# Wider zero rows from alternate partitions, and x and dy on two DMA queues, in a decode step with its gradients

## The chip, the cores and the metric

The kernel runs on one core of a Trainium2 chip. The metric is device time in microseconds (us), the median over runs of the whole program. The core has a matrix engine (PE), VectorE (DVE), ScalarE (ACT), GpSimd (POOL) and SyncE (SP), and 16 DMA engines that serve three queues here: SP's and ACT's (hardware queues, `q1` and `q10` in the profile) and POOL's (the software queue, `q0`).

## What is computed

One decode step of a parallel block, forward and backward. Four batch rows of width 512 are normalised. Attention with 32 query heads, 8 key/value heads of width 128 and a cache of 4096 positions uses only the last W = 1024 of them. A gated feed-forward part of width 1792 runs beside it.

```python
def _A_ref(x, k_cache, v_cache, wq, wo):
    W = min(4096, max(256, Sk // 4))
    q = (x @ wq).reshape(B, Sq, Hq, Dh)...
    k = jnp.repeat(k_cache[:, :, Sk - W:, :], rep, axis=1)
    v = jnp.repeat(v_cache[:, :, Sk - W:, :], rep, axis=1)
    p = _softmax(jnp.einsum("bhqd,bhkd->bhqk", q, k) * (Dh ** -0.5))
    o = jnp.einsum("bhqk,bhkd->bhqd", p, v)
    return ... @ wo
def _B_ref(x, w_gate, w_up, w_down):
    return (_gelu(x @ w_gate) * (x @ w_up)) @ w_down
xn = _layernorm(x)
out = x + _A_ref(xn, ...) + _B_ref(xn, ...)
# outputs: out, and the gradients of x, k_cache, v_cache, wq, wo, w_gate, w_up, w_down for grad_out
```

The gradients of the two caches have the caches' full shape (4 x 8 x 4096 x 128 in bf16); three quarters of them, the positions before the window, are zeros that the kernel has to write.

## The kernel before

**Head.** x and dy (the incoming gradient) are loaded by ACT's queue, each row repeated 32 times so that all 128 partitions are filled (L128). Layer norm on DVE and ACT gives `xn_b` and, through four PE transposes, `xnT`. `dyP` is a 32 x 32 block transpose of dy and is copied into `dyBD`, which PE later multiplies with. Small masks and selections (`hsel`, `hsel2`, `selp` and others) are made on DVE from the identity.

**Loads.** SP's queue issues the weights in the order `wg`, `wu`, `wd`, `wq`, `wo`, then the first key tile `ka`, then the first four zero transfers (L266 to L272). The later key and value tiles (`va`, `kb`, `ka`) are loaded from POOL's queue.

**Zeros.** `ztile` (128 partitions of 6 KB) is the source of all zeros. `zeros(n, after)` (L240) issues n transfers from SP's queue, each for two heads of one batch row of one gradient: 2 x 128 rows of 6 KB, 1.5 MB; 32 of them in all. A zero transfer waits for the one two before it, so that two are in flight, and, where `after` is given, for that instruction: the first 4 are free, and of the rest most wait for the landing of a key or value load (2 for `va` of batch 0, 3 for `kb` of batch 1, then 2 and 3 per batch, 4 for the last `va`), 3 for the last softmax and 6 for the last two attention products.

**Feed-forward part** (L253 to L375). `h_ps` = xnT times wg and wu; GELU and its derivative on DVE and ACT with fp32 values `x2`, `ua`, `th`, `h1` in tiles of the pool `ffn`; then the gradients `dwd`, `dwu`, `dwg`. Results are evacuated from PSUM into staging tiles (`stg_tile`, 4 buffers) by ACT or DVE, as `evac` (L82) chooses from a running cost of both, and stored from POOL's queue by `result` (L112).

**Attention** (L377 to L634). Per batch row: `scores` (DVE transposes a key or value tile through `scratch`, two buffers, and PE multiplies), `softmax`, `turned`, `odq` (product with the values, `od_ps`), the load of the next tile, `dvdk` (the gradient of the values or keys: 16 evacuations into two staging tiles, two stores of 1 MB). `get_d` (L452) uses `hsel` and `hsel2` as weights; `selh` is a selection used in `odq`, `selb` one used at the end.

**End** (L636 on). out, the gradient of x, and the gradients of wo and wq, four 1 MB stores each.

The engines' instruction order comes from a scheduler; SP's queue is scheduled by hand, in program order.

Of the kernel before, what the change touches and what calls it, by code (L numbers as in the profile page):

```python
# [11 lines left out]
FP32 = mybir.dt.float32  # L12
BF16 = mybir.dt.bfloat16
U32 = mybir.dt.uint32
P = 128
# [3 lines left out]
def kernel(  # L19
# [24 lines left out]
    nc = tc.nc  # L44

    B, Sq, D = A_x.shape
    _, G, Sk, Dh = A_k_cache.shape
# [4 lines left out]
    K0 = Sk - W  # L52
    F = B_w_gate.shape[1]
    Q = 32
    NQ = P // Q
# [5 lines left out]
    NPB = D // 64  # L61
# [8 lines left out]
    const = ctx.enter_context(tc.tile_pool(name="const", bufs=1))  # L70
# [20 lines left out]
    def t32(out, in_, n):  # L91
        load["dve"] += (130 + n) / 0.96
        nc.vector.transpose(out=out, in_=in_)  # L93

    def pairs(ap):
        return ap.bitcast(U32)

    def scratch():
        return scrp.tile([P, 1024], U32, name="scr", tag="scr")

    def stg_tile():
        return stage.tile([P, 4096], BF16, name="stg", tag="stg")

    def store(eng, out, in_, kind, apart, **kw):

        d = eng.dma_start(out=out, in_=in_, **kw)  # L106
        for k in apart:
            tc.declare_no_dep(d.ins, group=k, reason="stores write disjoint parts of the outputs")
        tc.add_to_no_dep_group(kind, d.ins)
        return d  # L110
# [4 lines left out]
    def mm(out, lhsT, rhs, first=True, last=True, pos=None):  # L115
        kw = {} if pos is None else {"tile_position": pos}
        nc.tensor.matmul(out, lhsT=lhsT, rhs=rhs, start=first, stop=last, **kw)  # L117

    def bank(name, tag="w", shape=(P, 512), dt=FP32):
        pool = {"w": ps_w, "x": ps_x}.get(tag, ps_a)  # L120
        return pool.tile(list(shape), dt, name=name, tag=tag)
# [3 lines left out]

    x_b = const.tile([P, D], BF16, name="x_b")
    dy_b = const.tile([P, D], BF16, name="dy_b")
    for dst, src in ((x_b, A_x), (dy_b, grad_out)):  # L128
        nc.scalar.dma_start(out=dst[:], in_=bass.AP(tensor=src.tensor, offset=src.offset,
                                                  ap=[[0, Q], [D, B], [1, D]]))  # L130

    ident = const.tile([P, P], BF16, name="ident")
    make_identity(nc, ident[:])
# [11 lines left out]
    r0 = rsum[:, 0, :]  # L145
# [3 lines left out]
    def mask(name, n, in_):  # L149
        t_ = const.tile([P, n], FP32, name=name)  # L150
        nc.vector.reduce_sum(out=t_[:], in_=in_, axis=AX.X)
        return t_
# [6 lines left out]
    hm = mask("hm", Q, ident_f[:].rearrange("p (h d) -> p h d", d=4))  # L159
# [5 lines left out]
    TS(out=oms[:], in0=om[:], scalar1=scale, scalar2=None, op0=ALU.mult)  # L165
    gmask_b = const.tile([P, G], BF16, name="gmask_b")
    nc.vector.tensor_copy(out=gmask_b[:], in_=gmask[:])
    hsel = const.tile([P, NQ, Q], BF16, name="hsel")
    nc.vector.tensor_copy(out=hsel[:], in_=hm[:].unsqueeze(1).broadcast_to([P, NQ, Q]))
    hsel2 = const.tile([P, NQ, 4, 8], BF16, name="hsel2")  # L170
    nc.vector.tensor_copy(out=hsel2[:], in_=hm[:].rearrange("p (c r) -> p c r", c=NQ).unsqueeze(2)
                          .broadcast_to([P, NQ, 4, 8]))
    rs2 = const.tile([P, NQ, 4, 8], FP32, name="rs2")
    for c in range(NQ):
        TS(out=rs2[:, c], in0=m8[:].unsqueeze(1).broadcast_to([P, 4, 8]), scalar1=bm[:, c:c + 1], scalar2=None,
# [3 lines left out]
    for a in range(4):  # L179
        TS(out=selp[:, a], in0=rs2[:, :, 0, :], scalar1=amask[:, a:a + 1], scalar2=None, op0=ALU.mult)  # L180

    ZW = K0 // P * Dh
    ztile = const.tile([P, ZW], BF16, name="ztile")
    nc.gpsimd.memset(ztile[:], 0.0)


    stats = const.tile([P, nc.vector.BN_STATS_DIM], FP32, name="stats")
# [13 lines left out]
        nc.tensor.transpose(tps[:, c, :], xn_b[0:Q, c:D:C], ident[0:Q, 0:Q])  # L201
    nc.vector.tensor_copy(out=xnT[:], in_=tps[:])

    dyP = const.tile([P, NPB, Q], U32, name="dyP")
    t32(dyP[:], pairs(dy_b[:]), 256)
    dyBD = const.tile([P, NPB, 2, P], BF16, name="dyBD")
    nc.gpsimd.memset(dyBD[:], 0.0)
    dyPb = dyP[:].bitcast(BF16).rearrange("p n (x r) -> p n r x", r=2)
    for q in quad:
        nc.vector.tensor_copy(out=dyBD[q, :, :, q], in_=dyPb[q])  # L210

# [17 lines left out]
        return d  # L229

    ZG = 2
    zsrc = bass.AP(tensor=ztile.tensor, offset=ztile.offset, ap=[list(ztile[:].ap[0]), [0, ZG], [1, ZW]])
    ztodo = [(og, b, g) for b in range(B) for g in range(0, G, ZG) for og in (out_2, out_3)]
    zdone = []

    def behind(ins, other):
        tc.add_manual_dep(ins, other.name,
                          mybir.DependencyInfo(mybir.DependencyClass.Sync, mybir.DependencyReason.DATA))

    def zeros(n, after=None):  # L240

        for _ in range(n):
            og, b, g = ztodo.pop(0)
            z = store(nc.sync, og[b, g:g + ZG, 0:K0, :].rearrange("g (m j) d -> m g (j d)", m=P), zsrc, "zeros",
                      ["rest"])
            if len(zdone) >= 2:
                behind(z.ins, zdone[-2].ins)
            if after is not None:
                behind(z.ins, after.ins)
            zdone.append(z)  # L250


    with tc.tile_pool(name="ffn", bufs=1) as ffn:  # L253
        wd_sb = ffn.tile([P, FB, D], BF16, name="wd_sb")

        def ft(name, dt=FP32):
            return ffn.tile([P, Q, FB], dt, name=name)
# [1 line left out]
        def flat(t_):  # L259
            return t_[:].rearrange("p f c -> p (f c)")  # L260

        hg, hu, x2, ua, th, h1, gl = (ft(n) for n in ("hg", "hu", "x2", "ua", "th", "h1", "gl"))
        a_b, dhu, dhg = (ft(n, BF16) for n in ("a_b", "dhu", "dhg"))
        wu_sb = ffn.tile([P, C, F], BF16, name="wu_sb")
        wg_sb = ffn.tile([P, C, F], BF16, name="wg_sb")
# [8 lines left out]
        for wsb, t_ in ((wg_sb, hg), (wu_sb, hu)):  # L274
            ps = bank("h_ps", "w", (P, FQ))
# [46 lines left out]
        for fb in range(FB):  # L322
            c = fb % 4
# [4 lines left out]
        for h in range(2):  # L328
            stg = stg_tile()
            for i in range(FB // 2):  # L330
                ps = bank("dwd_ps")
# [7 lines left out]
        for wi, (wsb, dh, og) in enumerate(((wu_sb, dhu, out_7), (wg_sb, dhg, out_6))):  # L339
            dh_f = flat(dh)  # L340
            dhr = stg_tile()
            for a, q in enumerate(quad):
                ps = bank("rep_ps", "w", (P, FQ))
# [9 lines left out]
            for ch in range(4):  # L353
# [5 lines left out]
                for k in range(n7):  # L359
                    for r in range(2):  # L360
                        c = nm % 4
# [4 lines left out]
            for h in range(2):  # L366
                stg = stg_tile()
                for ci in range(2):
                    for a, q in enumerate(quad):
                        ps = bank("dwg_ps", "w", (P, FQ))  # L370
# [6 lines left out]
    with tc.tile_pool(name="mid", bufs=1, reuse_waits="tile") as mid:  # L377
# [3 lines left out]
        selb = mid.tile([Q, 4, P], BF16, name="selb")  # L381
        with tc.tile_pool(name="att", bufs=1, reuse_waits="tile") as att:
# [7 lines left out]
            for k in range(2):  # L390
                bd.append([])
                for u in range(2):
                    t_ = att.tile([P, DPB, NQ, 2, 2, Q], BF16, name=f"bd{k}{u}")
                    nc.gpsimd.memset(t_[:], 0.0)
                    bd[k].append(t_)
            selh = att.tile([P, 4, Q, 4], FP32, name="selh")
            nc.gpsimd.memset(selh[:], 0.0)
            for d4 in range(4):
                nc.gpsimd.tensor_copy(out=selh[:, d4, :, d4], in_=r0)
            nc.gpsimd.tensor_copy(out=selb[:], in_=selh[0:Q].rearrange("p d h e -> p d (h e)"))  # L400
            nc.gpsimd.memset(dqs[:], 0.0)

            q_ps = bank("q_ps", "x", (P, Hq, B))
# [40 lines left out]
            for u in range(2):  # L444
                t32(doX[:, u * 16:(u + 1) * 16, :], do_ps[u][:], 512)
            d4mask = mask("d4mask", 4, r0.rearrange("p (g i) -> p i g", i=rep))
            dM = scratch()[:].bitcast(BF16)[:, 0:512].rearrange("p (b e k) -> p b e k", b=B, e=4)
            for d4 in range(4):
                TS(out=dM[:, :, d4, :], in0=doX[:, :, 0:B].rearrange("p k x -> p x k"), scalar1=d4mask[:, d4:d4 + 1],
                   scalar2=None, op0=ALU.mult)  # L450

            def get_d(ps, u):  # L452
                l_ = hsel[:].rearrange("p a h -> p (a h)") if u == 0 else hsel2[:].rearrange("p c a r -> p (c a r)")
                mm(ps[:].rearrange("p b d -> p (b d)"), l_, dM.rearrange("p b e k -> p (b e k)"))

            spread_rows(1, get_d)

            def refill(k, b):
# [104 lines left out]
            def odq(k, b, pT):  # L563

                ps = bank("od_ps", "x", (P, 2, Dh))
                src = (v_t, k_t)[k][b]
                for j in range(J):
                    for c, q in enumerate(quad):
                        mm(ps[q].rearrange("p g d -> p (g d)"), pT[:, j, :], src[:, 2 * c:2 * c + 2, j, :],
                           j == 0, j == J - 1, (0, Q * c))  # L570
                mk = (om, oms)[k]
                t_ = att.tile([P, Dh], FP32, name="odt", tag=f"odt{k}")
                nc.scalar.activation(out=t_[:], in_=ps[:, 0, :], func=ACT.Copy, scale=mk[:, 0:1])  # L573
                done = STT(out=t_[:], in0=ps[:, 1, :], scalar=mk[:, 1:2], in1=t_[:], op0=ALU.mult, op1=ALU.add)  # L574
                if k == 0:
                    ps = bank("ok_ps", "x", (P, NQ, 4, 2))
                    for d4 in range(4):
                        mm(ps[:].rearrange("p c t e -> p (c t e)"), selh[:, d4].rearrange("p h e -> p (h e)"),
                           t_[:, d4 * Q:(d4 + 1) * Q].rearrange("p (t c e) -> p c t e", t=4, c=NQ), d4 == 0, d4 == 3)
                    nc.vector.tensor_copy(out=oK[:, :, b], in_=ps[:].rearrange("p c t e -> p (c t e)"))  # L580
                else:
                    ps = bank("dqr_ps", "x", (P, Dh))
                    mm(ps[:], rsum_f, t_[:])
                    nc.scalar.copy(out=dqr[:, b, :], in_=ps[:])
                    d3 = att.tile([P, DPB, Q], U32, name="d3", tag="d3")
                    t32(d3[:], pairs(dqr[:, b, :]), 64)
                    d3v = d3[:].bitcast(BF16).rearrange("p e (h r) -> p h e r", r=2)
                    for a, q in enumerate(quad):
                        nc.vector.tensor_copy(out=dqs[q, :, :, :, a * B + b], in_=d3v[q])  # L589
                return done  # L590
# [45 lines left out]
        with tc.tile_pool(name="end", bufs=1, reuse_waits="tile") as end:  # L636
# [14 lines left out]
            for n in range(KH):  # L651
                t, e, c = n // 8, n // 4 % 2, n % 4
# [17 lines left out]
            for hc in range(8):  # L670
                for k in range(8):
                    for r in range(2):
                        c = nm % 4
# [38 lines left out]
            for t in range(4):  # L712
                stg = stg_tile()
                for e in range(2):
                    for c, q in enumerate(quad):
                        ps = bank("dwo_ps")
# [6 lines left out]
            for c in range(C):  # L723
                stg = stg_tile()
                for u in range(2):
                    for a, q in enumerate(quad):
                        ps = bank("dwq_ps")
# [34 lines left out]
```

## Time and profile before

| | |
|---|---|
| median of 3 runs | 288.5 us (287.89 to 289.36) |
| profiled execution | 287.67 us, of which the span of instructions is 285.9 us |
| mean granted PE clock | 0.623 |
| busy: PE, DVE, ACT, POOL | 64%, 57%, 43%, 21% of the span |
| DMA | 112.21 MB, mean 392 GB/s; 20979 packets |
| zeros (`out_dram<-ztile`) | 32 transfers of 1536 KB from SP's queue, median 12.7 us from issue to landing |
| stores (`out_dram<-stg`) | 24 of 1024 KB and 6 of 896 KB from POOL's queue, median 14.1 and 10.0 us |

In the profile, times are us from the span's start. A busy row gives an engine's time in instructions; the row DMA in 40 slices gives the mean busy share of the 16 DMA engines in tenths. The chain is the work that ended last, followed back from the last instruction through what released each step. In a timeline row the columns are start, length, engine, line, operation, result<-operands and, in brackets, the idle time before it and what ended it. "SPq", "ACTq" and "POOLq" are the engines' sequencers, where DMAs are issued; a DMA's issue is far shorter than the transfer.

### The profile page before, as it was taken

To read this page: it belongs to the slowest core of one execution; us is meant where nothing else is said; L and a number is where in the kernel's file an instruction comes from. 1 tells how busy PE (TensorE), PEld (TensorE's weight loads), DVE (VectorE), ACT (ScalarE), POOL (GpSimd) and SP (SyncE) were. 2 spreads that over 40 slices of the span, in tenths; PEclk is the share of its full clock that TensorE was granted. 3 is DMA by queue.
4 is the path that set the end of the run, shared out by engine and by line. 5 is a ranking of instruction groups with operands and counts; after the bars stand their busy time and mean duration, and the time that the engine had idled before them with its cause. 6 is when DMAs were issued, how large, how long until landed. Compare 5 with 4: busy or idle time off the path is not lost.

```text
span 285.9 us, 4404 instructions
## 1 busy us (share of the span) xinstructions
PE 183.3 (64%) x1731; PEld 75.1 (26%) x1733; DVE 161.8 (57%) x309; ACT 123.9 (43%) x245; POOL 60.6 (21%) x135
## 2 busy tenths in 40 slices
PE   0022689986935499869955697513769979755660
PEld 0010235423312252424321352201343234201110
DVE  0058975789979653457219553073974042775570
ACT  1004287382010248956823535303607593554560
POOL 8400001047618222313040060200200102011010
PEclk9999997555885555757555555555555575755555
DMA  7999999999999949999999999999999999999995
GB/s 273 420 462 435 398 380 423 419 426 369 390 424 425 376 161 410 378 357 421 407 418 376 423 415 406 420 424 419 403 399 395 414 386 399 391 406 412 415 402 220
DMA packets 20979, 112.21 MB, mean 392 GB/s; under 512 B 1368, under 2 KB 1632, under 8 KB 19296
## 3 DMA queue, kind: packets, MB, share of 16 engines
q1 hardware_dynamic: 10480, 66.32, 56.6%
q0 software_dynamic: 10176, 45.35, 40.6%
q10 hardware_dynamic: 304, 0.27, 0.3%
q8 instruction: 13, 0.21, 0.3%
q14 instruction: 6, 0.05, 0.0%
HBM read 30.93 MB, written 81.01 MB: 391 GB/s over the span
## 4 chain that ended last, share of the span: by engine, by line
PE 22%; DMA 22%; DVE 15%; ACT 4%; issue 4%; POOL 1%; POOLq 0%; DVEq 0%; ACTq 0%
DMA out_dram<-stg 16%; PE kv_ps L117 7%; DVE scr L93 6%; DMA va<-in_A_v_cache_dram 6%; ACT stg L88 3%; PE od_ps L117 3%; PE sc_ps L117 2%; PE ob_ps L117 2%; DVE stg L89 2%; DVE dqs L589 2%; PE dxq_ps L117 2%; DVE wq_sb L93 2%; PE ok_ps L117 1%; PE dwq_ps L117 1%; PE dwo_ps L117 1%
## 5 line engine op out<-in xcount | busy, mean ns | idle before, releaser
L88 ACT CAST stg<-kv_ps 128x512 bf16<-128x512 f32 x118 | 63.6, 605 | 42.3 <-PE kv_ps L117 21.6
L106 POOL DMA_DIRECT2D out_dram<-stg x30 | 19.8, 660 | 157.0 <-ACT stg L88 93.0
L117 PE MATMUL sc_ps<-scr,bd 128*32 128x256 bf16 x256 | 23.5, 391 | 16.3 <-DVE scr L93 16.3
L117 PE MATMUL kv_ps<-dm,spr 32*128 32x256 bf16 x128 | 28.0, 391 | 4.0 <-ACT stg L88 2.4
L117 PE MATMUL kv_ps<-qm,spr 32*128 32x256 bf16 x128 | 24.4, 371 | 7.4 <-ACT stg L88 6.9
L93 DVE STREAM_TRANSPOSE scr<-va 128x1024 uint32<-128x1024 uint32 x16 | 18.8, 1215 | 14.7 <-DMA va<-in_A_v_cache_dram 14.6
L117 PEld LDWEIGHTS <-spr 32*128 32x128 bf16 x256 | 12.2, 101 | 40.0 <-issue 35.6
L117 PEld LDWEIGHTS <-bd 128*32 128x32 bf16 x256 | 7.9, 108 | 27.7 <-issue 26.9
L88 ACT CAST stg<-dwg_ps 128x448 bf16<-128x448 f32 x26 | 12.6, 553 | 5.7 <-PE dwg_ps L117 4.8
L88 ACT CAST stg<-dwo_ps 128x512 bf16<-128x512 f32 x18 | 10.0, 589 | 11.5 <-PE dwo_ps L117 10.2
L117 PE MATMUL dwo_ps<-dy_b,oSP 32*128 32x512 bf16 x32 | 9.9, 549 | 6.8 <-ACT stg L88 5.9
L117 PE MATMUL dwq_ps<-dqSP,xn_b 32*128 32x512 bf16 x32 | 10.5, 588 | 5.8 <-ACT stg L88 5.3
L89 DVE CAST stg<-dwq_ps 128x512 bf16<-128x512 f32 x15 | 9.9, 689 | 6.4 <-DMA out_dram<-stg 3.4
L574 DVE SCALAR_TENSOR_TENSOR odt<-od_ps,oms,odt 128x128 f32<-128x128 f32 x4 | 1.4, 340 | 20.9 <-ACT odt L573 20.9
L89 DVE CAST stg<-kv_ps 128x512 bf16<-128x512 f32 x10 | 6.6, 678 | 10.4 <-PE kv_ps L117 7.4
L88 ACT CAST stg<-dwq_ps 128x512 bf16<-128x512 f32 x17 | 9.3, 587 | 6.4 <-DMA out_dram<-stg 4.5
L226 POOL DMA_DIRECT2D va<-in_A_v_cache_dram x8 | 6.0, 758 | 27.9 <-PE od_ps L117 27.9
L117 PE MATMUL do_ps<-scr,dyBD 128*128 128x512 bf16 x31 | 10.1, 458 | 2.4 <-DVE scr L93 2.0
L201 PE MATMUL tps<-ident,xn_b 32*128 32x32 bf16 x4 | 0.3, 194 | 17.5 <-DVE xn_b L197 17.5
L93 DVE STREAM_TRANSPOSE scr<-ka 128x1024 uint32<-128x1024 uint32 x8 | 9.6, 1228 | 2.3 <-PE sc_ps L117 1.6
L89 DVE CAST stg<-dwo_ps 128x512 bf16<-128x512 f32 x14 | 9.2, 679 | 2.7 <-PE dwo_ps L117 1.4
L117 PEld LDWEIGHTS <-pT 128*32 128x32 bf16 x256 | 9.3, 140 | 5.1 <-ACT pT L88 2.3
(197 smaller groups left out, 322.4 us busy)
## 6 DMA issues: line engine op xcount, KB each, us to landing
out_dram<-ztile SPq DMA_DIRECT2D x32, 1536.0 KB, 12.7
out_dram<-stg POOLq DMA_DIRECT2D x24, 1024.0 KB, 14.1
va<-in_A_v_cache_dram POOLq DMA_DIRECT2D x8, 1024.0 KB, 12.6
out_dram<-stg POOLq DMA_DIRECT2D x6, 896.0 KB, 10.0
wq_sb<-in_A_wq_dram SPq DMA_DIRECT2D x1, 4096.0 KB, 25.0
wo_sb<-in_A_wo_dram SPq DMA_DIRECT2D x1, 4096.0 KB, 33.8
kb<-in_A_k_cache_dram POOLq DMA_DIRECT2D x4, 1024.0 KB, 15.7
ka<-in_A_k_cache_dram SPq DMA_DIRECT2D x2, 1024.0 KB, 31.2
```

Source lines behind the costliest of these rows:

```text
L88: return nc.scalar.copy(out=out, in_=in_)
L89: return nc.vector.tensor_copy(out=out, in_=in_)
L93: nc.vector.transpose(out=out, in_=in_)
L106: d = eng.dma_start(out=out, in_=in_, **kw)
L117: nc.tensor.matmul(out, lhsT=lhsT, rhs=rhs, start=first, stop=last, **kw)
L201: nc.tensor.transpose(tps[:, c, :], xn_b[0:Q, c:D:C], ident[0:Q, 0:Q])
L226: d = eng.dma_start(out=tl[:, hs].rearrange("p g j d -> p g (j d)"), in_=src[b, hs, K0:Sk, :].rearrange("g (m j) d -> m g (j d)", j=J), **kw)
L574: done = STT(out=t_[:], in0=ps[:, 1, :], scalar=mk[:, 1:2], in1=t_[:], op0=ALU.mult, op1=ALU.add)
L589: nc.vector.tensor_copy(out=dqs[q, :, :, :, a * B + b], in_=d3v[q])
```

## The change

x is loaded from the head of SP's queue; dy stays on ACT's queue, alone. `ztile` holds 12 KB per partition, and a zero transfer reads 64 alternate partitions (0, 2, 4 and so on): 2 x 64 rows of 12 KB, the same 1.5 MB. The memory for this comes from tiles that go: the four fp32 feed-forward values share one staging tile, `dyP`, `hsel` and `hsel2` go into scratch tiles (the last two are now made just before their use), and `selh`, four selections of 128 columns, becomes one row pattern of 132 columns that is read at four offsets.

```diff
-    for dst, src in ((x_b, A_x), (dy_b, grad_out)):
-        nc.scalar.dma_start(out=dst[:], in_=bass.AP(tensor=src.tensor, offset=src.offset,
-                                                  ap=[[0, Q], [D, B], [1, D]]))
+    for eng, dst, src in ((nc.sync, x_b, A_x), (nc.scalar, dy_b, grad_out)):
+        eng.dma_start(out=dst[:], in_=bass.AP(tensor=src.tensor, offset=src.offset,
+                                              ap=[[0, Q], [D, B], [1, D]]))
...
-    hsel = const.tile([P, NQ, Q], BF16, name="hsel")
-    nc.vector.tensor_copy(out=hsel[:], in_=hm[:].unsqueeze(1).broadcast_to([P, NQ, Q]))
-    hsel2 = const.tile([P, NQ, 4, 8], BF16, name="hsel2")
-    nc.vector.tensor_copy(out=hsel2[:], in_=hm[:].rearrange("p (c r) -> p c r", c=NQ).unsqueeze(2)
-                          .broadcast_to([P, NQ, 4, 8]))
...
-    ZW = K0 // P * Dh
+    ZP = P // 2
+    ZW = K0 // ZP * Dh
     ztile = const.tile([P, ZW], BF16, name="ztile")
-    nc.gpsimd.memset(ztile[:], 0.0)
+    nc.gpsimd.memset(ztile[:].bitcast(FP32), 0.0)
...
-    dyP = const.tile([P, NPB, Q], U32, name="dyP")
-    t32(dyP[:], pairs(dy_b[:]), 256)
+    dyP = scratch()[:, 0:256].rearrange("p (n x) -> p n x", n=NPB)
+    t32(dyP, pairs(dy_b[:]), 256)
...
-    zsrc = bass.AP(tensor=ztile.tensor, offset=ztile.offset, ap=[list(ztile[:].ap[0]), [0, ZG], [1, ZW]])
+    zsrc = bass.AP(tensor=ztile.tensor, offset=ztile.offset, ap=[[2 * ztile[:].ap[0][0], ZP], [0, ZG], [1, ZW]])
...
-            z = store(nc.sync, og[b, g:g + ZG, 0:K0, :].rearrange("g (m j) d -> m g (j d)", m=P), zsrc, "zeros",
+            z = store(nc.sync, og[b, g:g + ZG, 0:K0, :].rearrange("g (m j) d -> m g (j d)", m=ZP), zsrc, "zeros",
...
-        hg, hu, x2, ua, th, h1, gl = (ft(n) for n in ("hg", "hu", "x2", "ua", "th", "h1", "gl"))
+        hg, hu, gl = (ft(n) for n in ("hg", "hu", "gl"))
+        tmp = stg_tile()[:, 0:4 * 2 * F // NQ].bitcast(FP32).rearrange("p (t f c) -> p t f c", t=4, f=Q)
+        x2, ua, th, h1 = (tmp[:, t] for t in range(4))
...
-            selh = att.tile([P, 4, Q, 4], FP32, name="selh")
+            selh = att.tile([P, P + 4], FP32, name="selh")
             nc.gpsimd.memset(selh[:], 0.0)
-            for d4 in range(4):
-                nc.gpsimd.tensor_copy(out=selh[:, d4, :, d4], in_=r0)
-            nc.gpsimd.tensor_copy(out=selb[:], in_=selh[0:Q].rearrange("p d h e -> p d (h e)"))
+            nc.gpsimd.tensor_copy(out=selh[:, 4:P + 4].rearrange("p (h e) -> p h e", e=4)[:, :, 0], in_=r0)
+            for b in range(B):
+                nc.gpsimd.tensor_copy(out=selb[:, b, :], in_=selh[0:Q, 4 - b:P + 4 - b])
...
-            dM = scratch()[:].bitcast(BF16)[:, 0:512].rearrange("p (b e k) -> p b e k", b=B, e=4)
+            dsc = scratch()[:].bitcast(BF16)
+            dM = dsc[:, 0:512].rearrange("p (b e k) -> p b e k", b=B, e=4)
+            hsel = dsc[:, 512:640].rearrange("p (a h) -> p a h", a=NQ)
+            hsel2 = dsc[:, 640:768].rearrange("p (c a r) -> p c a r", c=NQ, a=4)
+            nc.vector.tensor_copy(out=hsel, in_=hm[:].unsqueeze(1).broadcast_to([P, NQ, Q]))
+            nc.vector.tensor_copy(out=hsel2, in_=hm[:].rearrange("p (c r) -> p c r", c=NQ).unsqueeze(2)
+                                  .broadcast_to([P, NQ, 4, 8]))
```

More of the change, by code (lines that the diff above doesn't have):

```diff
@@ L202 @@
     nc.vector.tensor_copy(out=xnT[:], in_=tps[:])
-    dyP = const.tile([P, NPB, Q], U32, name="dyP")
-    t32(dyP[:], pairs(dy_b[:]), 256)
+    dyP = scratch()[:, 0:256].rearrange("p (n x) -> p n x", n=NPB)
+    t32(dyP, pairs(dy_b[:]), 256)
     dyBD = const.tile([P, NPB, 2, P], BF16, name="dyBD")
     nc.gpsimd.memset(dyBD[:], 0.0)
-    dyPb = dyP[:].bitcast(BF16).rearrange("p n (x r) -> p n r x", r=2)
+    dyPb = dyP.bitcast(BF16).rearrange("p n (x r) -> p n r x", r=2)
     for q in quad:
@@ L452, in get_d @@
             def get_d(ps, u):
-                l_ = hsel[:].rearrange("p a h -> p (a h)") if u == 0 else hsel2[:].rearrange("p c a r -> p (c a r)")
+                l_ = dsc[:, 512:640] if u == 0 else dsc[:, 640:768]
                 mm(ps[:].rearrange("p b d -> p (b d)"), l_, dM.rearrange("p b e k -> p (b e k)"))
@@ L577, in odq @@
                     for d4 in range(4):
-                        mm(ps[:].rearrange("p c t e -> p (c t e)"), selh[:, d4].rearrange("p h e -> p (h e)"),
+                        mm(ps[:].rearrange("p c t e -> p (c t e)"), selh[:, 4 - d4:P + 4 - d4],
                            t_[:, d4 * Q:(d4 + 1) * Q].rearrange("p (t c e) -> p c t e", t=4, c=NQ), d4 == 0, d4 == 3)
```

## The prediction

> **What bounds the kernel now.** I read the page's DMA rows first, since they say whether any engine matters at all. In the third section a row is a queue, its packets, its bytes and the time of its packets as a share of 16 engines' span.
>
> ```profile
> DMA  7999999999999949999999999999999999999995
> GB/s 273 420 462 435 398 380 423 419 426 369 390 424 425 376 161 410 378 357 421 407 418 376 423 415 406 420 424 419 403 399 395 414 386 399 391 406 412 415 402 220
> ...
> q1 hardware_dynamic: 10480, 66.32, 56.6%
> q0 software_dynamic: 10176, 45.35, 40.6%
> ```
>
> The two queues fill 97% of the DMA engines' span. So the time is bytes over rate plus the slices that aren't full: the first, the fifteenth and the last. Next I asked for busy time by stretch around the fifteenth.
>
> ```profile
> 90.00:100.00 10.00, 4.95 (x89) 2.63 (x85) 7.60 (x13) 1.85 (x5) 4.42 (x20) 0.50 0.95 394
> 100.00:107.00 7.00, 6.68 (x67) 4.35 (x66) 4.22 (x15) 3.01 (x6) 1.82 (x3) 0.50 0.43 148
> ```
>
> The last columns are clock, DMA share and GB/s. From 100 to 107 us the engines lie idle for 7.0 x (1 - 0.43) = 4.0 us: the permitted zeros have landed, and the next transfer, the load of `va` for batch 1, is issued at 102.57, after `od_ps` of batch 0. Compute was late there; elsewhere transfers are. The chain in order of time says which transfers compute waits for:
>
> ```profile
> 131.52 17.89 DMA va<-in_A_v_cache_dram
> ...
> 167.97 31.63 DMA out_dram<-stg
> ...
> 254.27 13.92 DMA out_dram<-stg
> ```
>
> Last, the timeline of the head, for why compute is late.
>
> ```profile
> 0.82 0.62 ACTq L129 DMA_DIRECT2D x_b<-in_A_x_dram  x1
> ...
> 1.47 0.61 ACTq L129 DMA_DIRECT2D dy_b<-in_grad_out_dram  x1
> ...
> 11.26 0.70 DVE L188 BATCH_NORM_STATS2 stats<-x_b 128x6 f32<-128x512 bf16 x1 [10.09 <-DMA x_b<-in_A_x_dram]
> ...
> 15.94 0.45 DVE L93 STREAM_TRANSPOSE dyP<-dy_b 128x256 uint32<-128x256 uint32 x1 [3.98 <-DMA dy_b<-in_grad_out_dram]
> ...
> 19.90 1.68 PE L117 MATMUL h_ps<-wg_sb,xnT 128*32 128x448 bf16 x16 [2.11 <-DVE xnT L202]
> ```
>
> x takes 10.4 us, dy 14.4, and VectorE's order puts dy's transpose ahead of the rest of the layer norm: the first matmul waits for dy.
>
> **The head: 8 us of lead.** x's 128 KB lead SP's queue. The nearest row is `wg`, which headed that queue: issued at 0.81, all 1792 KB landed 7.5 us later, first packet in the records 1.6 us after issue. So x lands at about 3.5. dy becomes first on ACT's queue. It lands at 3.5 at the soonest, and at 11.2 at the latest, which is x's old landing from that very place. I take 5, since x's rows are short and `wg` is now issued behind both. VectorE's stretch from dy's transpose to `xnT` is 15.94 to 19.84; two casts of `hsel` leave it (0.2 each), so about 3.6, and `xnT` stands at 8.6. `wg` comes one issue (0.45) later, at 0.81 + 7.5 + 0.45 = 8.8, so the first matmul moves from 19.90 to 8.8; `wu` is there at 1.26 + 11.7 + 0.45 = 13.4 for a matmul that ran at 21.37. The lead is thus 8 to 11 us, and 4.7 (15.9 - 11.2) if dy is late. I carry 8. Weights for later (`wq` 27, `wo` 37, `ka` 42 us) land far ahead of their uses at 43, 67 and 82, so the lead should survive.
>
> [...]
>
> **What the lead is worth: 4.0 us.** Not 8, because the DMA engines are full before 100 us and after 107. With more than 4.5 us of lead the `va` load is issued before the last permitted zeros have landed, and the hole closes: -4.0 us. At 4.7 it just does; with no lead, 0.
>
> **12 KB rows: -1.9 us.** Zeros are 32 transfers of 256 rows, 8192 of q1's packets; 4096 go. The packet records give a median 234 ns for 6 KB and 1216 ns for 32 KB: 36.9 ns per KB (1000 B), so 7.4 ns of each packet isn't bytes, and 4096 x 7.4 / 16 engines = 1.9 us. Bounds: the two queue rows (247 ns for 6.33 KB, 182 for 4.46 on average) give 28.7 ns a packet, 7.3 us; the other way, no row shows a source of 64 partitions, and the slowest rate of large rows in SP's queue is that of `ka`'s 2 KB rows, 91 ns each. The zeros at that rate take 50.3 MB / (16 x 22.4 KB per us) = 140.3 us of all engines instead of 122.6 (8192 x 239.5 ns / 16): +17.7. I take the 1.9, because the 32 KB rows are nearest in kind.
>
> [...]
>
> **Shares: +1.4 us.** When both queues have work, the engines take one packet of each in turn: 166 zeros of 6 KB beside 165 packets of 4 KB in 4 us of records near 165 us. In the SP queue's own rows the zeros go out every 6.2 us:
>
> ```profile
> 193.63 0.37 SPq L106 DMA_DIRECT2D out_dram<-ztile  x1
> ...
> 199.83 0.37 SPq L106 DMA_DIRECT2D out_dram<-ztile  x1
> ```
>
> That is 1.573 MB / 6.2 = 254 of 416 GB/s, 61%; POOL's stores get 162. With 12 KB against 4 KB zeros get 75%, 312 GB/s, and POOL 104. A load that zeros wait for is unhurt: its landing still needs the same sum of permitted bytes. Stores are hurt. After the last `va` lands (187.3) four zeros are permitted, 6.3 MB or 20 us at 312; the 2.1 MB of stores that the chain waits for until 199.7 (12.4 us) then also need 20. So the evacuations, behind them on ScalarE and VectorE the last softmax, come up to 7.6 us later. Meanwhile the DMA engines have the stores issued at 180, so they don't idle, and zeros used early aren't left for the end, where the chain still loses 13.9 us to stores. From there DMA needs 98.6 us (to 285.9) and compute, by 44 us (207 to 251) and eight stores of some 2.8, would end at about +100: 1.4 us past. Bounds 0 and 7.6.
>
> **The rest: 0.** The casts of `hsel` and `hsel2` now stand in the chain at 81 us (two of 0.22), covered by the lead; without it 0.4. The memset of `ztile` writes as many elements, twice the bytes (2.66 us now; `selh`'s 512 fp32 took 0.55, so 3.3 at most), 0.7 later for the memsets behind it on POOL, whose tiles are needed after 12 us. SP's queue starts the weights 0.45 us later while x's bytes move. `selh` and `selb` are POOL work of 1.8 us in all, before an 8.1 us wait. The feed-forward values take one of the four staging tiles, and the first `dwg` evacuation (43.30) reuses it, 1.3 us after its last reader (dhg, 42.04); all other tiles wait for what they waited for.
>
> **Sum.** -4.0 - 1.9 + 1.4 = -4.5 us on a span of 285.9, in an execution of 287.67 (1.8 around the span), which lies 0.8 under the median of 288.5. So 288.5 - 4.5 = 284.0. The likeliest case's own range is 279.5 (rows save 5, shares cost nothing) to 287.
>
> **Rivals.**
> Zero rows that read slower (chance 0.22). Place: every zero transfer, 45% of all bytes. For it: no row has such a source. Against it: rows of 14 and 32 KB ran at the best rates. It decides when a zero byte gets 3.7% dearer (4.5 of 122.6 us); at the 2 KB rows' rate the time is 288.5 - 4.0 + 17.7 + 1.4 - 2 (fewer shares lost), about 301.6. Slower.
> Stores starved by zeros (0.12): the whole 7.6 lands on the chain, 288.5 - 5.9 + 7.6 = 290.2. For it: the 31.6 us wait. Against it: zeros are metered by loads. It decides above 5.9 us. Slower.
> The head doesn't move (0.10): dy's transpose stays ahead and dy stays late, or the lead is lost to the feed-forward part's staging tiles; the hole remains, 288.5 - 1.9 + 1.4 = 288.0. Same.
> Forecast (0.56).
>
> **How the numbers follow.** About 0.5% (1.4 us) is what a measurement here can tell from no change. Faster: the forecast, 0.56. Same: 0.10 and a little of the starved case, 0.11. Slower: 0.33. The range 279.5 to 301.6 takes in the forecast, the same and starved cases, and the slow rows up to the price that rows give them; beyond it lie about half of the slow rows and a few hundredths below.
>
> **What would show it.** x landing near 3.5 and the first `h_ps` matmul near 9; no slice under 9 around 100 us; q1 with 6384 packets and a smaller share (about 55.9% of this span's length); zeros 5 us apart when stores run beside them; the wait for stores near 190 us longer. Wrong: zeros alone further apart than now (89.80 to 93.39 in the SP rows, 3.6 us), a q1 share that grows, or a `va` load still issued after 100.

## The result, and the profile after

The changed kernel takes 313.12 us (median of four runs, 312.47 to 314.69), against 288.93 us (median of four) for the kernel before: a ratio of 1.083 (95% interval 1.079 to 1.087). The forecast was 284.0 us and faster; 313 lies above the whole range of 279.5 to 301.6. The profiled execution took 313.36 us, its span 311.4.

The page's DMA rows after (busy tenths in 40 slices of 7.8 us, rate in each slice, then the two large queues with packets, MB and share of 16 engines):

```profile
DMA  6999999999999999999999999470065799999997
GB/s 229 431 451 429 344 416 422 427 414 396 427 398 385 372 391 313 427 407 407 377 423 425 420 376 419 168 269 3 34 238 209 316 419 413 418 418 424 417 426 316
q1 hardware_dynamic: 6528, 66.46, 51.9%
q0 software_dynamic: 10176, 45.35, 37.1%
```

The hole of the fifteenth slice is gone, as forecast. A far larger one stands in slices 26 to 32, down to 3 GB/s. The stretches of that hole and of the end (after their bounds and length: busy us of PE, its weight loads, DVE, ACT and POOL, then clock, DMA share, GB/s):

```profile
184.00:243.00 59.00, 47.95 (x499) 19.88 (x497) 30.98 (x60) 32.04 (x67) 6.02 (x8) 0.52 0.53 204
...
275.00:311.00 36.00, 0.00 (x0) 0.00 (x0) 0.00 (x0) 0.00 (x0) 0.00 (x0) 0.50 0.96 403
```

For 59 us the engines compute as ever while the DMA engines are idle for 59 x (1 - 0.53) = 27.7 us. From 275 us no engine computes any more: what is left is zeros and the last stores. So the bytes were not slower; they came late. SP's queue says where it stood, in its timeline and, for the DMAs it later waits for, ACT's:

```profile
184.17 0.60 SPq L106 DMA_DIRECT2D out_dram<-ztile  x1
...
243.27 1.25 SPq L106 DMA_DIRECT2D out_dram<-ztile  x2
...
255.28 1.49 SPq L106 DMA_DIRECT2D out_dram<-ztile  x2
...
302.82 0.60 SPq L106 DMA_DIRECT2D out_dram<-ztile  x1
```

```profile
239.66 0.53 ACTq L669 DMA_DIRECT2D out_dram<-out_b  x1
...
250.38 0.26 ACTq L707 DMA_DIRECT2D out_dram<-dx_b  x1
```

No zero is issued from 184.77 to 243.27, though the conditions that the source names for them were met long before: the zero two before, the last `va` (landed by 187.6, where DVE starts to transpose it), the last softmax (done at 202.6). The table of SP's waits (waiter, what it waited for: us in all, times, longest) names the reason:

```profile
SPq L106 <- DMA out_dram<-ztile: 138.8, 24, 16.8
SPq L106 <- DMA out_dram<-out_b: 58.4, 1, 58.4
...
SPq L106 <- DMA out_dram<-dx_b: 6.3, 1, 6.3
```

A zero waits 58.4 us for the 4 KB store of `out`, which ACT issues at 239.66, and a later one waits for the store of `dx`. Nothing in the source makes a zero wait for either. The records of the two traces show where the waits come from. In each, the 43 DMAs of SP's and of ACT's queue name eight completion semaphores between them, in one round over both queues: 100, 102, 103, 105, 107, 108, 117, 118, and 100 again (POOL's DMAs name 109 to 116). In the changed kernel the store of `out` and zero 21 both name 118: its last update from the store is at 243.20, SP's record of the wait for it at 243.22, zero 21 at 243.27. The store of `dx` and zero 23 both name 102: last update at 255.26, zero 23 at 255.28. Counting the zeros from 1, with the numbers named:

| | before | after |
|---|---|---|
| place of the store of `out` in the round | 107, between zeros 27 (105) and 28 (108) | 118, between zeros 14 (117) and 15 (100) |
| place of the store of `dx` in the round | 118, between zeros 29 (117) and 30 (100) | 102, between zeros 15 (100) and 16 (103) |
| next zero with the number of `out`, of `dx` | none, none | 21, 23 |

The times agree: 12 of the 32 zeros are issued from 243.27 on, so the one that stood was the 21st, and the second stand, to 255.28, was before the 23rd. Zeros 21 to 32 thus stood behind two stores that depend on nearly the whole computation.

The profile of before showed such a wait once, harmlessly, in a view that the prediction did not use, SP's waits:

```profile
SPq L226 <- DMA x_b<-in_A_x_dram: 7.0, 1, 7.0
```

Why would a key load on SP wait for x on ACT's queue? x, dy, five weights and the first half of `ka` are eight DMAs; the second half of `ka` is the ninth, and names 100 as x did. The last update of 100 from x is at 11.23, and that half is issued at 11.25.

### The profile page after: what moved, and what is told of

It reads as the page before. It is cut to its first block, busy times and chain, and to the rows that moved or that the text cites. A ratio compares the mean times of both kernels' runs of the same rounds, so it can differ in the third digit from the quotient of the medians.

```text
span 311.4 us, 4405 instructions
## 1 busy us (share of the span) xinstructions
PE 186.2 (60%) x1731; PEld 76.3 (24%) x1733; DVE 164.6 (53%) x309; ACT 124.5 (40%) x245; POOL 60.4 (19%) x135
## 3 DMA queue, kind: packets, MB, share of 16 engines
q1 hardware_dynamic: 6528, 66.46, 51.9%
## 4 chain that ended last, share of the span: by engine, by line
DMA 23%; PE 16%; DVE 15%; issue 5%; ACT 3%; POOL 1%; POOLq 0%; DVEq 0%; ACTq 0%
DMA out_dram<-stg 13%; DMA va<-in_A_v_cache_dram 11%; DVE scr L93 7%; PE kv_ps L117 5%; ACT stg L88 2%; DVE stg L89 2%; PE od_ps L117 2%; PE dwo_ps L117 2%; PE ob_ps L117 2%; DVE dqs L593 2%; PE sc_ps L117 2%; PE dxq_ps L117 1%; DVE wq_sb L93 1%; POOL va L222 1%; DVE spr L492 1%
## 5 line engine op out<-in xcount | busy, mean ns | idle before, releaser
L117 PE MATMUL sc_ps<-scr,bd 128*32 128x256 bf16 x256 | 24.6, 401 | 18.8 <-DVE scr L93 18.8
L117 PE MATMUL kv_ps<-dm,spr 32*128 32x256 bf16 x128 | 28.9, 399 | 10.2 <-ACT stg L88 8.6
L117 PE MATMUL dwo_ps<-dy_b,oSP 32*128 32x512 bf16 x32 | 9.1, 509 | 6.0 <-ACT stg L88 4.5
L93 DVE STREAM_TRANSPOSE scr<-kb 128x1024 uint32<-128x1024 uint32 x8 | 9.8, 1230 | 4.5 <-DMA kb<-in_A_k_cache_dram 3.9
L93 DVE STREAM_TRANSPOSE scr<-wo_sb 128x1024 uint32<-128x1024 uint32 x8 | 9.7, 1233 | 1.2 <-PE do_ps L117 1.1
```

## The experiments

Three theories stood after the comparison; the expectations call them A, B and C. **A, semaphores:** the stall is the re-use just told, and moving the two small stores off ACT's queue removes it. **B, rows:** the 12 KB rows in themselves slow or starve the other transfers. **C, order:** the head's lead has brought the scheduler to an order in which the end is late. The same change of one word is made in several kernels; the diffs show it once.

**Both small stores from POOL's queue** (`e1_after_pool_out`; `e4_before_pool_out` is the same edit in the kernel before):

```diff
-            nc.scalar.dma_start(out=out_0.rearrange("b s d -> (b s) d"), in_=out_b[:])
+            nc.gpsimd.dma_start(out=out_0.rearrange("b s d -> (b s) d"), in_=out_b[:])
...
-            nc.scalar.dma_start(out=out_1.rearrange("b s d -> (b s) d"), in_=dx_b[:])
+            nc.gpsimd.dma_start(out=out_1.rearrange("b s d -> (b s) d"), in_=dx_b[:])
```

> The changed kernel, with the two small stores (out and the gradient of x, 4 KB each) issued from POOL's queue and not from ACT's; nothing else is changed. Theory A (SP's queue stood from 185 to 243 us because zero 21 waits for the completion semaphore that the 4 KB store of out was given, and zero 23 for that of the gradient of x): the stall goes, no slice of the DMA row is under 8 between 100 and 270 us, time 279 to 286 us. Rival B (the 12 KB zeros themselves cost it, by starving POOL's transfers or reading slowly): the time stays at 305 to 314. Rival C (the head's lead has brought the scheduler to an order in which the end is late): 300 or more.

> The kernel before, with the two small stores issued from POOL's queue. Control for the move itself: no zero waited for them before, so all theories expect 287 to 290 us.

Measured: 285.33 us, ratio to before 0.985 (0.979 to 0.990). Three views follow: the second part of the hole in the changed kernel, then the DMA row of e1's page, then the same window in e1.

```profile
212.00:243.00 31.00, 29.50 (x314) 11.02 (x315) 9.05 (x26) 20.63 (x41) 3.02 (x4) 0.54 0.37 136
```

```profile
DMA  6999999999999999999999999999999989999995
```

```profile
212.00:243.00 31.00, 28.16 (x276) 10.49 (x269) 10.33 (x27) 18.45 (x36) 2.95 (x4) 0.56 0.98 398
```

Two 4 KB stores on another queue are worth 313.12 - 285.33 = 27.8 us (28.3 by the two ratios, which compare each kernel with the one before in its own series), near the 27.7 us of idle DMA. In the kernel before the same edit gives 290.27 us, 0.3 over its expected range, 1.002 (0.998 to 1.005): POOL's queue is not better in itself; there was nothing to remove.

**6 KB rows from all partitions, the rest of the change kept** (`e2_after_6k_rows`):

```diff
-    ZP = P // 2
+    ZP = P
...
-    zsrc = bass.AP(..., ap=[[2 * ztile[:].ap[0][0], ZP], [0, ZG], [1, ZW]])
+    zsrc = bass.AP(..., ap=[list(ztile[:].ap[0]), [0, ZG], [1, ZW]])
```

> The changed kernel with the zero rows of before: 128 partitions of 6 KB (the tile keeps its 12 KB, of which half is read); x and dy, the tiles and the stores as changed. Theory A: without the 64-partition transfers the two small stores get their semaphores late in the order, as before the change, so no stall: 281 to 287 us. Rival B: the same, 281 to 287. Rival C: 300 or more.

**The old head, the rest kept** (`e3_after_old_head`):

```diff
-    for eng, dst, src in ((nc.sync, x_b, A_x), (nc.scalar, dy_b, grad_out)):
+    for eng, dst, src in ((nc.scalar, x_b, A_x), (nc.scalar, dy_b, grad_out)):
```

> The changed kernel with x and dy both on ACT's queue, as before; 12 KB rows from 64 partitions kept. Theory A: zero 21 still shares its semaphore with the store of out, so SP's queue stalls from about 185 until that store has landed: 310 to 320 us. Rival B: 300 to 318, with no wait of SP for the store of out. Rival C: 286 to 290.

Measured: with 6 KB rows 287.57 us, 0.6 over its expected range, 0.989 (0.984 to 0.994), no wait for `out`; with the old head 315.49 us, 1.088 (1.081 to 1.095), and SP's waits hold

```profile
SPq L106 <- DMA out_dram<-out_b: 56.7, 1, 56.7
```

So the rows' edit brings the stall and the head's does not, and C falls. The programs of the two runs say the same: the store of `out` has its place in the round between zeros 27 and 28 with 6 KB rows, between 14 and 15 with the old head. Why the scheduler places the two stores earlier when a zero reads 64 partitions was not shown.

**The stall's two halves** (`e9_only_out_moved`, `e10_only_dx_moved`): one of e1's two edits each.

> The changed kernel with only the store of out on POOL's queue; the gradient of x stays on ACT's. Theory A: one semaphore fewer is taken early, zero 23 (not 21) is the one that shares with a small store, the gradient of x, which is issued some 10 us later than out. SP then stands before zero 23 until about 253 us, with 10 zeros (15.7 MB) and 8.4 MB of stores left, 24 MB or 58 us at 415 GB/s: end at some 311, time 309 to 315 us. If the wait were of another kind (an order of the queues, starved stores), moving one of two stores should bring about half of the first experiment's gain: 297 to 302.

> The changed kernel with only the gradient of x stored from POOL's queue; out stays on ACT's. Theory A: zero 22 (not 21) shares with the store of out; SP stands until out has landed, about 243 us, with 11 zeros (17.3 MB) and 8.4 MB of stores left, 62 us: end at some 306, time 305 to 310 us, between the changed kernel and the one with the store of out moved only in place, not in price. The other kind of wait: 297 to 302.

Measured: 316.73 us, 1.091 (1.085 to 1.097), and 311.56 us, 1.073 (1.068 to 1.079). SP's waits in the one and in the other:

```profile
SPq L106 <- DMA out_dram<-dx_b: 57.0, 1, 57.0
```

```profile
SPq L106 <- DMA out_dram<-out_b: 59.9, 1, 59.9
```

Each store alone blocks the stream, at the zero that its place in the round names: 23 with `dx` left on ACT's queue (issued at 257.79, 63 us after zero 22) and 22 with `out` left (245.25). Both times came out above their expected ranges, by 1.7 and 1.6 us; the stands ended at 257.8 and 245.3, where about 253 and 243 were expected.

**Both small stores at the end of SP's queue** (`e11_stores_on_sp`): `nc.scalar` becomes `nc.sync`, which puts them behind the last zero.

> The changed kernel with both small stores issued from SP's queue, where the program order puts them behind the last zero: no zero can wait for them, and they need no place among POOL's stores. Theory A: as the first experiment, 283 to 287 us, with SP's wait for its own zeros only. If leaving POOL's queue or ACT's mattered by itself, this differs from the first experiment by over 3 us.

Measured: 286.19 us, 0.985 (0.981 to 0.989), no wait for `out`. In its program they still name two of the eight semaphores (102 and 103, behind the 100 of zero 32), but no zero comes after them. What hurt is a late store placed among the zeros, not the queue that the others use.

**The parts without the stall** (`e6_head_alone`: e1's edits and 6 KB rows; `e7_rows_alone`: e1's edits and the old head; `e5_pool_out_again`: e1 once more). All three keep the edits of the tiles, which no run takes out by themselves.

> The changed kernel with both small stores on POOL's queue once more, beside the next two on one chip, so that the parts of the change can be told apart without the stall. Prediction's sum (-4.5 us on 288.5): 283 to 286 us, ratio about 0.985. A theory in which 12 KB zeros starve the stores at a price: ratio over 0.99.

> Both small stores on POOL's queue and zero rows of 6 KB from 128 partitions again: what is left is the head (and the tiles). The prediction's terms give the hole's 4.0 us to the head: ratio about 0.986. If the rows carry the gain (larger packets), it is 0.995 or more here.

> Both small stores on POOL's queue and both small loads on ACT's queue as before: what is left is the 12 KB rows. The prediction's terms give -1.9 + 1.4 us: ratio about 0.998, and DMA idle again between 100 and 107 us. If the rows carry the gain, 0.99 or less.

Measured, as ratios to before:

| head | rows | small stores on ACT's queue | on POOL's queue |
|---|---|---|---|
| old | 6 KB | 1 | 1.002 (0.998 to 1.005) |
| new | 6 KB | 0.989 (0.984 to 0.994) | 0.987 (0.981 to 0.994) |
| old | 12 KB | 1.088 (1.081 to 1.095) | 0.997 (0.993 to 1.001) |
| new | 12 KB | 1.083 (1.079 to 1.087) | 0.985 (0.980 to 0.990) |

The first row is the kernel before, without the edits of the tiles; the other rows have them, so they stand in both parts. In the right column the parts add up: 0.987 x 0.997 = 0.984. The window of the old hole, in e7 and then in e5:

```profile
100.00:107.00 7.00, 6.05 (x103) 4.33 (x103) 4.02 (x10) 3.57 (x8) 2.50 (x6) 0.50 0.20 53
```

```profile
100.00:107.00 7.00, 6.87 (x67) 1.89 (x65) 1.94 (x7) 4.94 (x10) 0.92 (x4) 0.50 0.99 368
```

With the old head the hole is back (DMA share 0.20), with the new one it is closed (0.99).

**Zeros from the first 64 partitions** (`e8_first_64`), to see whether the rival of slow rows had a basis at all:

```diff
-    zsrc = bass.AP(..., ap=[[2 * ztile[:].ap[0][0], ZP], [0, ZG], [1, ZW]])
+    zsrc = bass.AP(..., ap=[[ztile[:].ap[0][0], ZP], [0, ZG], [1, ZW]])
```

> As the first experiment, but the 12 KB zero rows are read from partitions 0 to 63 instead of 64 alternate ones. [...] If 64 partitions of either kind do as well, 284 to 287.

Measured: 390.95 and 396.94 us in two runs, the lower of them 105 us above e5, where 284 to 287 was expected if 64 partitions of either kind do as well. The packet records give a median of 919 ns for 12 KB (mean 862) where e1 has 460 (mean 472). By the means, 4096 packets x 390 ns / 16 engines = 100 us, near the loss. The page shows the DMA engines busy throughout, at a lower rate:

```profile
DMA  7999999999999999999999999999999998999996
GB/s 279 445 435 371 417 268 247 270 307 380 225 212 318 271 283 281 413 273 256 345 280 245 258 280 326 251 241 238 245 252 238 222 240 254 202 239 235 336 392 267
...
q1 hardware_dynamic: 6528, 66.46, 67.1%
```

A busy share of 9 stands here over rates from 202 to 445 GB/s, so it is the rate row that shows the loss. Measured a packet: 12,288 B from 64 partitions in a row in 919 ns, from 64 alternate ones in 460 ns, where 6 KB from all 128 partitions took 234 in the kernel before. What in the chip makes the difference was not shown.

## Why the prediction was wrong

**The step that failed** is "The rest: 0", in the words "all other tiles wait for what they waited for". It went through the tiles and the conditions of `zeros`, and took the waits that the source names for all the waits there are. The eight semaphores that SP's and ACT's DMAs share in the traces had no term, and their order moved: +27.8 us. The step could have been taken from the profile of before: SP's waits have the one row that no line of the source explains.

**The other terms held.** With the stall taken away, the change gives 0.985 x 288.5 = 284.2 us (interval 282.5 to 285.7), where the sum was 284.0. That they lie 0.2 apart is in part luck: the parts are known to within 1 or 2 us.

- The hole, -4.0: `e6_head_alone` measures 0.987, about -3.7 us (interval -1.8 to -5.5).
- Rows -1.9 and shares +1.4, -0.5 together: `e7_rows_alone` measures 0.997, -0.9 us (interval -1.9 to +0.2). No run separates these two terms, and the working of the +1.4 reaches its "about +100" only if the 13.9 us that the chain still loses to stores are added to the 20, the 44 and the eight times 2.8 (86 us without them). The packets take 460 ns, as 7.4 + 453 said. Beside stores the zeros of e1 go out 4.9 us apart at 192.91 and 197.78 and 5.0 to 5.5 us apart from 217.81 to 233.72, against the 5.0 forecast and 6.2 before. The chain's wait for stores grew from 31.63 to 35.57 us, half of the 7.6 that bounded it:

```profile
166.05 35.57 DMA out_dram<-stg
```

- The head, 8 us of lead: x's statistics start at 3.74 (forecast 3.5) and dy's transpose at 4.35 (forecast 5). The packet records show what changed. Before, x's 128 rows of 1 KB took from 5.63 to 10.28, in turn with 129 weight packets of 14 KB, and dy's rows followed to 14.93 beside 134 more. After, both were through by 3.40, and the first weight packet started at 3.34. dy left from ACT's queue both times. So these rows point to the place ahead of the weights, and not to the queue, as what counted; no run separates the two. Why x's first packet before came only 4.8 us after its issue at 0.82 they don't show. (The first packet of `wg` before started 1.0 us after its issue, and not 1.6.) The first `h_ps` matmul came at 11.56 and not at 8.8. The term of 3.6 us from the transpose to `xnT` was mis-sized: it measured 7.2 (4.35 to 11.51). Its durations came from a stretch of before (15.94 to 19.84) with no POOL memset in it, the last of the head having ended at 10.41; after, `xn_b` and `ident_f` ran beside such memsets and took 3.1 us more between them. Two rows of the head before, then the head after:

```profile
17.00 0.41 DVE L197 TENSOR_SCALAR xn_b<-x_b,mv,rstd 128x512 bf16<-128x512 bf16 x1
17.33 0.22 DVE L135 CAST ident_f<-ident 128x128 f32<-128x128 bf16 x1
```

```profile
3.74 0.69 DVE L184 BATCH_NORM_STATS2 stats<-x_b 128x6 f32<-128x512 bf16 x1 [2.58 <-DMA x_b<-in_A_x_dram]
...
5.40 2.03 DVE L193 TENSOR_SCALAR xn_b<-x_b,mv,rstd 128x512 bf16<-128x512 bf16 x1
...
5.49 1.80 POOL L203 MEMSET dyBD<- 128x2048 bf16 x1
...
7.23 1.73 POOL L290 MEMSET aSP<- 128x1792 bf16 x1
7.36 1.69 DVE L135 CAST ident_f<-ident 128x128 f32<-128x128 bf16 x1
...
11.56 1.69 PE L117 MATMUL h_ps<-wg_sb,xnT 128*32 128x448 bf16 x16 [3.76 <-DVE xnT L198]
```

  The lead was 19.90 - 11.56 = 8.3 us at the first matmul, as carried in the sum (8.8 would have made it 11), and still 102.57 - 95.12 = 7.45 us at the load of `va` for batch 1; 4.5 would have done.

**The rivals.** "Zero rows that read slower" comes nearest to the direction, but alternate partitions read no slower (460 ns for 12 KB, against twice 234 for 6 KB before); e8 shows the loss real for adjacent ones (919 ns). "Stores starved" is there at half its price. "The head doesn't move" is refuted by x at 3.74. None of the three contained the stall: two had the sign, for another reason.

**The signs named.** x, the hole, the pace of zeros and the wait for stores came out as forecast, in the changed kernel or in e1; the matmul in part. Of the signs of being wrong, zeros alone went out no further apart (91.41 and 94.99, 3.6 us), and the `va` load was issued before 100. The sign for q1 was off twice: 6528 packets and not 6384, since x's 144 moved onto that queue, and e1's packets of q1 took 56.8% of 283.4 = 161.0 us, 0.8 less than before (56.6% of 285.9 = 161.8) where the 1.9 of the rows was expected; as a share of e1's shorter span it grew, which the prediction names as a sign of being wrong. All these signs test the terms, not the sum; the list held none for SP's own waits.

## What to carry to other kernels

Here a bulk stream on one hardware queue stood 58.4 us behind a tiny, late DMA on the other, through a completion semaphore that both named. So after any change of a transfer's shape or place, read that queue's own waits and ask of every row which line of the source put it there. Keep DMAs that end late off the queues whose semaphores the stream cycles through, or behind the whole stream on its own queue: both gave 0.985 here, faster than either kernel. A sum whose terms hold can still miss by a wait that belongs to no term; the place to look for it in the profile of before is the row that nothing in the code explains.

## What the runs showed of the hardware

- Sixty-four partitions are not one thing: 12 KB from every second partition took 460 ns, from partitions 0 to 63 919 ns, and the kernel 105 us more.
- Two VectorE operations that ran beside POOL memsets took 5 to 8 times as long (`xn_b` 0.41 to 2.03 us, `ident_f` 0.22 to 1.69 us) and ended 0.14 and 0.09 us after that memset. Not all do: x's statistics ran beside the memset of `ztile` in 0.69 us, against 0.70 before. No run here moved the memsets, so the cause was not shown.
- A small load issued just ahead of the weights, and not with them, landed far sooner: x at 3.7 instead of 11.2 us. Among weight packets of 14 KB its 128 rows took 4.65 us (5.63 to 10.28), ahead of them 0.7 (2.71 to 3.40).
